# Gate and beta rows as broadcast loads behind the first weights, and an order planned with another table of load times

## The chip, the cores and the metric

The kernel runs on one core of one Trainium2 chip. The metric is the device time of one execution in microseconds, the median of several runs. Five engines take part: PE (TensorE, matrix products), DVE (VectorE), ACT (ScalarE), POOL (GpSimd) and SP (SyncE, which here issues nearly all DMAs).

## The reference, cut to what matters

The input `x` has 2048 tokens of width 512. The output mixes two branches token by token with a gate:

```
g = sigmoid((x * gate_w).sum(-1))            # one number for each token
a = A(x)        # attention with a memory, 32 heads of 16, four segments of 512 tokens
b = ((x @ W_gate) * (x @ W_gate > 0) * (x @ W_up)) @ W_down      # width 1792 between
out = g * a + (1 - g) * b
```

In each segment, branch A does causal attention within the segment (softmax of `q k / 4`), and from the second segment on reads a memory: `a_mem = phi(q) M / (phi(q) z + 1e-6)`. Here `M` and `z` are sums over the earlier segments of `phi(k) v` and `phi(k)`, and `phi(t)` is `t + 1` where `t > 0` and `exp(t)` elsewhere. The two are mixed by `sigmoid(beta)`, one number for each head, and then multiplied by `wo`.

So the gate row `gate_w` (512 numbers) is needed on all 128 partitions, since tokens lie on partitions when a token's gate is summed up; `beta` (32 numbers) is needed on all partitions too.

## The kernel before, in words

Everything stays in SBUF. The tokens are taken in four segments `s` of 512. For each there are projections (`proj`: `q`, `k` and `v`, four groups of four full 128x128x512 matmuls each), attention (`att`), memory update and reading (`mu`, `nd`), the two wide products with `W_gate` and `W_up` (`ffn`, 14 blocks of 128 columns) and the output product (`outp`), which adds up the attention part (`wo`) and the wide part (`wd`) in one accumulator.

`att` computes scores in groups called quads: matmuls that use the array as four row tiles of 32 and write all four banks of the PSUM tensor `psL`. One `exp` on ACT then turns the four banks into a tile of `E`, and POOL masks its diagonal blocks. The values (`pv`) use row tiles of 64 and write two banks of the other PSUM tensor, `psA`. Four banks of `psA` serve all accumulators; each is taken by a group of matmuls and is free again once its reader on DVE or ACT has copied it out.

The order of the work is not written down by hand. `program` describes every operation as an `Op` with the names that it reads and writes, a duration in nanoseconds and sometimes an earliest time (`after`). `Sched` then plays the work through with these durations and fixes, engine by engine, the order in which it is emitted and the semaphores that each instruction waits for. What counts for the change:

- `Sched.place` gives the time at which it believes that a DMA has landed. Operations that read the data are ready from then on.
- `Sched.jitter` adds a pseudo-random offset to the readiness of each operation, from a seed. The seeds change with PE's planned time, so each choice of seeds is another order.
- An engine executes its instructions in the emitted order. What is planned too early waits in its place, and what stands behind it waits too.

The names that the change touches: `touch` loads a few bytes early; `load` queues a weight load on SP or ACT; `load_gu(0)` and `load_gu(1)` load the first and second halves of the columns of `W_gate` and `W_up` (8 loads of 224 KB each); `load_x(c)` loads and transposes segment `c` of `x` into `xT`. `wo` and `wd` are loaded later, in one DMA each. `braw` holds `beta`, and `eb`, `romgh` and others are made of it. `gwb` is the gate row on 128 partitions.

In the kernel before, the gate row comes by a one-row DMA on ACT's queue into `oTt`. A matmul with a column of ones (`gwx`, L590) writes it to all partitions of a bank of `psL`, and ACT copies it to `gwb` (`gwc`, L592). The gates of segment 0 are four reductions on DVE (L620) that read the tiles `hT0` to `hT3`, which hold rows of `x` in the beginning. For the later segments a row tile is loaded into `osb` (`ldxr`, L625) and reduced (L628), one after the other, since they share a buffer. From a segment's four sums come `gexp` and `omg` on ACT and DVE; `gexp` is written to DRAM (`gscr`) and read back in another layout (`gexpT`, four DMAs), which `rdg` (L829) needs ahead of each attention output.

Other lines that the prediction names: L484 is the line of all plain loads, L506 of the transposing loads of `x`, L549 to L581 transpose segment 0, L655 is the exp of `phi`, L673 the `q` and `k` products, L671 `v`, L696 the transposes of `phik`, L721 adds up the memory, L743 to L745 read it, L757 makes `vsh` (a copy of the values shifted by 64 partitions), L775 are the quads, L781 the exps, L786 the masks, L809 the value products, L819 their transposes (`Tn`), L874 the wide products, L882 and L883 their relu (`rl`) on ACT or DVE, L885 the product that gives `hT`, L906 and L913 the output products.

Of the kernel before, what the change touches and what calls it, by code (L numbers as in the profile page):

```python
# [8 lines left out]
ACT = mybir.ActivationFunctionType  # L9
# [4 lines left out]

LAT = 60.0
MU_G = 1
PE_LAT = 175.0
SWITCH = 100.0
GATE_T = {1: 44000.0, 2: 90000.0, 3: 140000.0}
# [13 lines left out]

def t_pool(n, rate=1.0):
    return 160.0 + 0.975 * n * rate


PORT = ("kmask", "qts", "kts", "qphi", "kphi", "rdg", "ad", "oa", "gate", "omg1", "vone", "romgh", "epsv", "pmb")
# [59 lines left out]
class Sched:  # L98
# [178 lines left out]
    def place(self, op, e, start):  # L277
        op.eng = e
        if op.ep is not None and op.role == "w" and op.ep.bank is None:
            for ep in op.ep.group:  # L280
                bi, _ = self._bank_choice(op, e)
                for i in range(bi, bi + ep.nb):
                    if self.bank_ep[i] is not None:
                        op.preds += [(r, False) for r in self.bank_ep[i].readers]
                    self.bank_ep[i] = ep
                ep.bank = bi
        if e == "pool" and self.yield_to is not None:
            op.preds.append((self.yield_to, False))
            self.yield_to = None
        deps = {}  # L290
        for p in self._pred_done(op, e):
            deps[p.stream] = max(deps.get(p.stream, 0), p.idx)
        self._waits(e, deps)
        occ = op.occs[e]
        op.base = occ
        if e == "dve" and op.port:
            if self.pool_from <= start < self.now["pool"]:
                occ += self.now["pool"] - start
                self.yield_to = op
            self.port_free = start + occ  # L300
        if e == "pool":
            if start > self.now["pool"] + 1.0:
                self.pool_from = start
        if e == "pe":
            if op.mode != self.mode or start > self.now[e] + 60.0:
                occ += SWITCH
            self.mode = op.mode
        if op.dma:
            d = min(range(self.ndma), key=lambda i: (self.dma_end.get(i, 0.0), i))
            st = f"dma{d}"  # L310
            if self.cnt[st] > 0:
                self._waits(e, {st: self.cnt[st]})
            self.cnt[st] += 1
            self.semval[st, self.cnt[st]] = self.semval.get((st, self.cnt[st] - 1), 0) + 16 * op.nd
            inc = 16
            issued = start + occ
            self.dma_busy = max(self.dma_busy, issued) + op.nbytes / 340.0
            op.end = self.dma_busy + (1400.0 if start < 16000.0 else 5200.0 if start < 60000.0 else 3200.0)
            self.dma_end[d] = op.end
        else:  # L320
            st = e
            self.cnt[st] += 1
            inc = 1
            op.end = start + occ + op.lat
        idx = self.cnt[st]
        self.prog[e].append(("ins", op, st, inc))
        op.stream, op.idx, op.start, op.done = st, idx, start, True
        sn = dict(self.know[e])
        sn[st] = max(sn[st], idx)
        self.snap[st][idx] = sn  # L330
        self.now[e] = start + occ
        self.busy[e] += occ
        self.log.append((start, start + occ, e, op.name))
# [1 line left out]
    TOL = {"pe": 400.0, "act": 150.0, "dve": 250.0, "pool": 300.0, "sp": 300.0}  # L335

    def jitter(self, op):
        seed = self.seeds[min(int(self.now["pe"] / 34000.0), len(self.seeds) - 1)]
        j = self.jit.get((op.cidx, seed))
        if j is None:  # L340
            j = self.jit[op.cidx, seed] = random.Random(seed * 100003 + op.cidx).random() * 400.0
        return j

    def _choose(self, e):
# [15 lines left out]
        now = self.now[e]  # L360
        rdy = [h for h in heads if h[1] <= now + 20.0]
        if rdy:
            best = min(rdy, key=lambda h: (h[0], h[1] + self.jitter(h[2])))
            return best[2], best[1]
        hmin = min(heads, key=lambda h: (h[1], h[0]))
        best = hmin
# [60 lines left out]
def build_kernel(nc, A_x, A_wq, A_wk, A_wv, A_wo, A_beta, W_g, W_u, W_d, gate_w, out):  # L427
    _, S, D = A_x.shape
    F = W_g.shape[1]
    assert D == 512 and S % 512 == 0 and F % 128 == 0  # L430
    NSEG, KT, NF, NT = S // 512, D // 128, F // 128, S // 128
    EPS, SCALE = 1e-6, 16 ** -0.5
    sc = Sched(seeds=(52936,98560,17166,30259,57195,44848,1710,92264))
    T = {}
    with contextlib.ExitStack() as stack:
        for name, shape, dt in plan(S, D, F):
            T[name] = stack.enter_context(nc.sbuf_tensor(name, shape, dt))
        PL = stack.enter_context(nc.psum_tensor("psL", [128, 4, 512], F32))
        PA = stack.enter_context(nc.psum_tensor("psA", [128, 4, 512], F32))
        for st in sc.streams:  # L440
            sc.sem[st] = stack.enter_context(nc.semaphore(f"s_{st}"))
        program(sc, nc, T, PL, PA, A_x, A_wq, A_wk, A_wv, A_wo, A_beta, W_g, W_u, W_d, gate_w, out, NSEG, KT, NF, NT, EPS, SCALE)
        with nc.Block() as block:
            sc.emit(block)
    return sc


def program(sc, nc, T, PL, PA, A_x, A_wq, A_wk, A_wv, A_wo, A_beta, W_g, W_u, W_d, gate_w, out, NSEG, KT, NF, NT, EPS, SCALE):
# [31 lines left out]

    lact, lsp = [], []

    def load(eng, names, dst, src, nbytes, occ=460.0):
        (lact if eng == "act" else lsp).append(dma(eng, lambda e, dst=dst, src=src: e.dma_start(dst, src), nbytes, occ=occ, writes=names, name="ld" + names[0]))  # L484
    x0 = A_x[0, 0:512, :].rearrange("(i p) d -> p i d", p=128)
    def touch(n, src):
        load("act", ["adT"], V.adT[0:16, 32 * n:32 * n + 32], src, 1024)
    touch(0, A_wq[0:16, 0:32])
    load("act", ["oTt"], V.oTt[0:1, :], gate_w.rearrange("(a n) -> a n", a=1), 1024)
    for i in range(4):  # L490
        load("sp", [f"hT{i}"], V.hT[:, i, :], x0[:, i, :], 1 << 17)
    for nm, w, src in (("wq", V.wq, A_wq), ("wk", V.wk, A_wk), ("wv", V.wv, A_wv)):
# [11 lines left out]
    def load_x(c):  # L504
        for kt in range(KT):
            lsp.append(dma("sp", lambda e, c=c, kt=kt: e.dma_start_transpose(V.xT[:, kt, c * 512:(c + 1) * 512], A_x[0, c * 512:(c + 1) * 512, kt * 128:(kt + 1) * 128]),  # L506
                           1 << 17, occ=1280.0, writes=[f"xT{c}_{kt}"], name=f"ldx{c}_{kt}"))
    load("sp", ["braw"], V.braw[:], A_beta.partition_broadcast(128), 8192)
    load_gu(0)
    load_gu(1)  # L510
    load_x(1)
    sc.queue(0, lact)
# [19 lines left out]
    st = []  # L532
# [54 lines left out]
            ins = e.matmul(A(epw)[:, 0:n], lhsT=nc.const_aps.tensor(1.0, [128, 128], BF16), rhs=nc.const_aps.tensor(1.0, [128, n], BF16), start=True, stop=True)  # L587
        return ins
    xps.append(pe(warm1, 380, name="warm1", ep=epw, role="w"))
    xps.append(pe(lambda e: e.matmul(PL[:, 2, :], lhsT=nc.const_aps.tensor(1.0, [128, 128], BF16)[0:1, :], rhs=V.oTt[0:1, :], start=True, stop=True), 300, reads=["oTt"], writes=["bankL2"], name="gwx"))  # L590
    xps[-1].after = 6400.0
    xcs.append(act(lambda e: e.activation(V.gwb[:], PL[:, 2, :], ACT.Copy), t_act(512), reads=["bankL2"], writes=["gwb"], name="gwc"))  # L592
    sc.queue(0, xps)
    sc.queue(0, [t for t in xcs if t.eng == "dve"])
    sc.queue(0, [t for t in xcs if t.eng == "act"])
# [112 lines left out]
    def mu(s):  # L708
# [3 lines left out]
        def fn(e):  # L712
# [4 lines left out]
                                       rhs=V.vaug[:, s % 2, tt, 8 * G + 2 * j:8 * G + 2 * j + 2, :].rearrange("q h c -> q (h c)"),  # L717
                                       start=(tt == 0), stop=(tt == 3), tile_position=(0, 32 * j), skip_group_check=True)
            return ins
        m = pe(fn, 300.0, reads=[f"phik{g}" for g in range(4)] + va(s), name=f"mu{s}", ep=ep, role="w", mode="c")  # L720
        d = dve(lambda e: e.tensor_tensor(V.Mc[:], V.Mc[:], A(ep)[:, 0:136].rearrange("q (g c) -> q g c", g=4), ALU.add), t_dve(136), reads=["Mc"], writes=["Mc"], name=f"mum{s}", ep=ep, role="r")  # L721
        ps = []
        for G in range(4):
# [305 lines left out]
```

## Time and profile before

| what | value |
|---|---|
| median of 3 runs | 264.92 us (264.72, 264.92, 266.2) |
| profiled execution | 264.76 us, its span 263.0 us |
| PE busy | 254.4 us, 97% of the span, 2714 matmuls |
| ACT, DVE, POOL busy | 188.7, 181.5, 119.5 us |
| DMA | 19.23 MB, mean 73 GB/s; 135 to 379 GB/s in the first 33 us |
| granted TensorE clock | full speed |

The span is what the profiler sees from the first to the last record; the 1.8 us beside it are start and end of the execution. PE's busy time counts matmuls whose ends are modelled, so it is read for where it has holes, not for its rate. The records of a few matmuls are missing from the trace, mostly the first after a change of form. In a group's line the columns are: line, engine, operation, output <- input, count; in a timeline: start, duration, engine, line, operation, and in brackets the idle time ahead and what ended it.

### The profile page before, as it was taken

What the parts mean: (1) busy time and instruction counts of PE and PEld (TensorE: products, weight loads), DVE (VectorE), ACT (ScalarE), POOL (GpSimd) and SP (SyncE); (2) the same over time, 40 slices, a digit from 0 to 9 for tenths busy, and PEclk for the clock granted to TensorE, in tenths of its full rate; (3) what the DMA queues carried; (4) which work ended last, traced back from release to release, by engine and by line L of the source; (5) the groups of instructions that cost most, each with busy time, mean ns of one, the idle gap of its engine ahead of it and who ended that gap; (6) DMA issues with size and microseconds to landing.
All of it is one profiled execution on the core that took longest, in us unless ns stands there. A gap on an engine that the chain in (4) does not pass through costs nothing.

```text
span 263.0 us, 6637 instructions
## 1 busy us (share of the span) xinstructions
PE 254.4 (97%) x2714; PEld 113.1 (43%) x2748; DVE 181.5 (69%) x359; ACT 188.7 (72%) x167; POOL 119.5 (45%) x283
## 2 busy tenths in 40 slices
PE   7999999999999999999999999999999999999996
PEld 3444444434444443534444434444444434344444
DVE  5788887977886388876887954868582636657600
ACT  4597898599878789588886777787677657767021
POOL 3025544764545366764446265634344453535100
PEclk9999999999999999999999999999999999999999
DMA  6899666982041341510032320100034120000011
GB/s 182 223 379 209 135 83 80 286 146 57 20 106 23 75 68 44 82 40 4 0 87 64 80 62 23 21 4 2 0 92 55 22 60 22 0 2 1 4 40 40
DMA packets 34528, 19.23 MB, mean 73 GB/s; under 512 B 24001, under 2 KB 33986, under 8 KB 34498
## 3 DMA queue, kind: packets, MB, share of 16 engines
q1 hardware_dynamic: 34368, 18.80, 32.0%
q8 instruction: 21, 0.34, 0.6%
q14 instruction: 9, 0.07, 0.1%
q10 hardware_dynamic: 130, 0.01, 0.0%
HBM read 9.75 MB, written 2.11 MB: 45 GB/s over the span
## 4 chain that ended last, share of the span: by engine, by line
PE 94%; issue 2%; DVE 1%; DMA 1%; SPq 0%; ACT 0%; DVEq 0%
PE psA L874 37%; PE psA L913 19%; PE psA L673 11%; PE psL L775 9%; PE psA L809 7%; PE psA L906 5%; PE psA L671 5%; PE psA L736 1%; DMA hT<-in_A_x_dram 1%; PE psA L716 1%; DVE vaug L699 0%; SPq L484 0%; DVE phiq L657 0%; ACT xT L581 0%; DVE osb L922 0%
## 5 line engine op out<-in xcount | busy, mean ns | idle before, releaser
L786 POOL TENSOR_SCALAR_AFFINE_SELECT E<-E 64x256 bf16<-64x256 bf16 (+1 forms) x256 | 111.8, 446 | 122.2 <-ACT E L781 100.9
L781 ACT ACTIVATE E<-psL 128x2048 bf16<-128x2048 f32 x72 | 135.1, 1876 | 33.8 <-PE psL L775 31.1
L874 PE MATMUL psA<-xT,wg 128*128 128x512 bf16 x212 | 57.0, 380 | 1.9 <-issue 1.6
L874 PE MATMUL psA<-xT,wu 128*128 128x512 bf16 x219 | 58.0, 380 | 0.7 <-issue 0.5
L913 PE MATMUL psA<-wd,hT 128*128 128x512 bf16 (+2 forms) x229 | 52.2, 366 | 1.1 <-issue 1.0
L885 DVE TENSOR_TENSOR hT<-psA,rl 128x512 bf16<-128x512 f32 x56 | 38.2, 681 | 13.6 <-PE psA L874 11.3
L819 DVE STREAM_TRANSPOSE Tn<-psA 128x512 f32<-128x512 f32 x32 | 21.3, 696 | 20.0 <-PE psA L809 20.0
L913 PEld LDWEIGHTS psA<-wd,hT 128*128 128x128 bf16 x238 | 21.4, 98 | 23.7 <-issue 1.9
L874 PEld LDWEIGHTS psA<-xT,wu 128*128 128x128 bf16 x224 | 20.6, 98 | 25.3 <-issue 1.5
L874 PEld LDWEIGHTS psA<-xT,wg 128*128 128x128 bf16 x224 | 20.0, 98 | 24.9 <-issue 3.9
L775 PE MATMUL psL<-qT,kp 32*128 32x192 bf16 (+7 forms) x512 | 28.5, 287 | 0.0
L882 ACT ACTIVATE rl<-psA 128x512 bf16<-128x512 f32 x32 | 19.1, 597 | 10.2 <-PE psA L874 9.5
L775 PEld LDWEIGHTS psL<-qT,kp 32*128 32x128 bf16 x512 | 8.2, 92 | 29.9 <-issue 15.3
L923 ACT ACTIVATE osb<-psA,omg 128x512 bf16<-128x512 f32 (+1 forms) x12 | 8.1, 679 | 17.9 <-PE psA L906 14.0
L883 DVE TENSOR_SCALAR rl<-psA 128x512 bf16<-128x512 f32 x24 | 16.7, 696 | 3.2 <-PE psA L874 2.5
L809 PE MATMUL psA<-E,vaug 64*17 64x128 bf16 (+7 forms) x512 | 18.7, 283 | 0.0
L809 PE MATMUL psA<-E,vsh 64*17 64x128 bf16 (+7 forms) x512 | 18.3, 283 | 0.0
L673 PE MATMUL psA<-xT,wq 128*128 128x512 bf16 x62 | 16.2, 380 | 0.5 <-ACT xT L581 0.3
L906 PE MATMUL psA<-wo,oT 128*128 128x512 bf16 (+2 forms) x67 | 16.2, 366 | 0.2 <-issue 0.2
L673 PE MATMUL psA<-xT,wk 128*128 128x512 bf16 x61 | 16.0, 380 | 0.4 <-issue 0.3
L671 PE MATMUL psA<-wv,xT 128*128 128x512 bf16 x62 | 14.7, 380 | 0.3 <-issue 0.3
L809 PEld LDWEIGHTS psA<-E,vaug 64*17 64x17 bf16 x512 | 11.6, 86 | 6.0 <-issue 3.6
(76 smaller groups left out, 214.9 us busy)
## 6 DMA issues: line engine op xcount, KB each, us to landing
vsh<-vaug SPq DMA_DIRECT2D x8, 272.0 KB, 3.8
out_dram<-osb SPq DMA_DIRECT2D x15, 128.0 KB, 1.7
wg<-in_B_W_gate_dram SPq DMA_DIRECT2D x8, 224.0 KB, 5.7
wu<-in_B_W_up_dram SPq DMA_DIRECT2D x8, 224.0 KB, 5.9
wd<-in_B_W_down_dram SPq DMA_DIRECT2D x1, 1792.0 KB, 10.0
osb<-in_A_x_dram SPq DMA_DIRECT2D x12, 128.0 KB, 2.2
hT<-in_A_x_dram SPq DMA_DIRECT2D x4, 128.0 KB, 2.4
wq<-in_A_wq_dram SPq DMA_DIRECT2D x4, 128.0 KB, 2.8
```

Of the source, the lines that this page charges most:

```text
L671: ins = e.matmul(A(ep)[:, :], lhsT=V.xT[:, kt, tok + col * 128:tok + (col + 1) * 128], rhs=w[:, kt, :], start=(kt == 0), stop=(kt == KT - 1))
L673: ins = e.matmul(A(ep)[:, :], lhsT=w[:, kt, col * 128:(col + 1) * 128], rhs=V.xT[:, kt, tok:tok + 512], start=(kt == 0), stop=(kt == KT - 1))
L775: ins = q.matmul(PL[:, jj, o:o + 512 - 64 * c], lhsT=V.kp[r, kslot(s, G), c, :], rhs=V.qT[r, qslot(s, G), 64 * c:512], start=True, stop=Tr ...
L781: acts.append(act(lambda a: a.activation(V.E[:, e, :, :], PL[:, :, :], ACT.Exp, scale=SCALE), t_act(2048), reads=[f"bankL{b}" for b in ran ...
L786: pools.append(pool(lambda g, ap=ap, base=base: g.affine_select(out=ap, in_=ap, compare_op=ALU.is_ge, fill=0.0, base=base, pattern=[[0, 4] ...
L809: ins = q.matmul(A(eps[p])[32 * jj:32 * jj + 17, 64 * c:512], lhsT=v[:, 8 * G + 2 * jj + p, :], rhs=V.E[r, e, jj, o:o + 512 - 64 * c], sta ...
L819: ds.append(dve(lambda e, p=p, ep=eps[p]: e.transpose(V.Tn[:, p, :], A(ep)[:, :]), t_dve(512), writes=[f"Tn{p}"], name=f"tr{s}_{G}_{p}", e ...
L874: ins = e.matmul(A(ep)[:, :], lhsT=w[:, kt, f * 128:(f + 1) * 128], rhs=V.xT[:, kt, c * 512:(c + 1) * 512], start=(kt == 0), stop=(kt == K ...
L882: evs.append(sc.add(Op([("act", lambda e, ep=eg, r=r: e.activation(V.rl[:, r, :], A(ep)[:, :], ACT.Relu), t_act(512)), ("dve", lambda e, e ...
L885: evs.append(dve(lambda e, ep=eu, r=r, hs=hs: e.tensor_tensor(V.hT[:, hs, :], A(ep)[:, :], V.rl[:, r, :], ALU.mult), t_dve(512), reads=[f" ...
L906: ins = e.matmul(A(ep)[:, 0:c1 - c0], lhsT=V.oT[:, o0 + G, i * 128:(i + 1) * 128], rhs=V.wo[:, G, c0:c1], start=st_ and G == 0, stop=sp_ a ...
L913: ins = e.matmul(A(ep)[:, 0:c1 - c0], lhsT=V.hT[:, slots[f], i * 128:(i + 1) * 128], rhs=V.wd[:, f, c0:c1], start=st_ and f == f0, stop=sp ...
```

## The change

It does three things. The one-row load, the matmul L590 and the copy L592 go; instead the gate row is loaded with one DMA that reads it for each of the 128 partitions. This DMA and that of `beta` stand behind the eight loads of `load_gu(0)`, where `beta`'s stood ahead of them. And the planner gets other numbers: a table `dma_time` with a service time and a latency for each kind of DMA, by which a load counts as landed 0.25 us after its service, in place of a rate with 1.4, 5.2 or 3.2 us on top; 490 in place of 300 ns for `mu`, 472 in place of 460 ns for an issue; sixteen seeds for 17 us each instead of eight for 34 us; and, for one operation in ten, an offset to its priority too. So from about 13 us on the whole emitted order is another one, with the same operations.

```diff
+STRETCH = 17000.0
+BUMP = 2.2
+BUMP_P = 0.1
...
+def dma_time(op):
+
+    n = op.name
+    for px, svc, lat in (("ldhT", 546, 1650), ("ldwq", 546, 1650), ("ldwk", 546, 1650), ("ldwv", 546, 1650), ("ldwg0_0", 1400, 1650), ("ldwg", 596, 1650), ("ldwu", 596, 1650),
+                         ("ldbraw", 1600, 1650), ("ldgwb", 1000, 1650), ("ldxr", 400, 1700), ("ldx", 560, 2000), ("kT2", 560, 2000), ("aT", 560, 2000), ("vsh", 850, 2300),
+                         ("ldwo", 1750, 1650), ("ldwd", 6100, 1650), ("st", 400, 1400), ("gwr", 50, 1700), ("grd", 100, 1900)):
+        if n.startswith(px):
+            return svc, lat
+    return op.nbytes / 300.0, 1650
...
-            self.dma_busy = max(self.dma_busy, issued) + op.nbytes / 340.0
-            op.end = self.dma_busy + (1400.0 if start < 16000.0 else 5200.0 if start < 60000.0 else 3200.0)
+            svc, lat = dma_time(op)
+            self.dma_busy = max(self.dma_busy, start + lat) + svc
+            op.end = self.dma_busy + (0.0 if start < 8000.0 else 250.0)
...
     def jitter(self, op):
-        seed = self.seeds[min(int(self.now["pe"] / 34000.0), len(self.seeds) - 1)]
+        seed = self.seeds[min(int(self.now["pe"] / STRETCH), len(self.seeds) - 1)]
         j = self.jit.get((op.cidx, seed))
         if j is None:
-            j = self.jit[op.cidx, seed] = random.Random(seed * 100003 + op.cidx).random() * 400.0
+            r = random.Random(seed * 100003 + op.cidx)
+            j = self.jit[op.cidx, seed] = (r.random() * 400.0, BUMP if r.random() < BUMP_P else 0.0)
         return j
...
-            best = min(rdy, key=lambda h: (h[0], h[1] + self.jitter(h[2])))
+            best = min(rdy, key=lambda h: (h[0] + self.jitter(h[2])[1], h[1] + self.jitter(h[2])[0]))
...
-    sc = Sched(seeds=(52936,98560,17166,30259,57195,44848,1710,92264))
+    sc = Sched(seeds=(20535,46112,39258,56108,387,36564,95759,69596,46532,65787,16279,44074,61783,45860,67077,4305))
...
-    def load(eng, names, dst, src, nbytes, occ=460.0):
+    def load(eng, names, dst, src, nbytes, occ=472.0):
...
     touch(0, A_wq[0:16, 0:32])
-    load("act", ["oTt"], V.oTt[0:1, :], gate_w.rearrange("(a n) -> a n", a=1), 1024)
...
+    load_gu(0)
     load("sp", ["braw"], V.braw[:], A_beta.partition_broadcast(128), 8192)
-    load_gu(0)
+    load("sp", ["gwb"], V.gwb[:], gate_w.partition_broadcast(128), 1 << 17)
     load_gu(1)
...
-    xps.append(pe(lambda e: e.matmul(PL[:, 2, :], lhsT=nc.const_aps.tensor(1.0, [128, 128], BF16)[0:1, :], rhs=V.oTt[0:1, :], start=True, stop=True), 300, reads=["oTt"], writes=["bankL2"], name="gwx"))
-    xps[-1].after = 6400.0
-    xcs.append(act(lambda e: e.activation(V.gwb[:], PL[:, 2, :], ACT.Copy), t_act(512), reads=["bankL2"], writes=["gwb"], name="gwc"))
...
-        m = pe(fn, 300.0, reads=[f"phik{g}" for g in range(4)] + va(s), name=f"mu{s}", ep=ep, role="w", mode="c")
+        m = pe(fn, 490.0, reads=[f"phik{g}" for g in range(4)] + va(s), name=f"mu{s}", ep=ep, role="w", mode="c")
```

Lines behind the table stand 13 to 16 higher in the new file: the quads are L788 there, the `q` and `k` products L686, the reductions of later segments L641.

## The prediction, made before the changed kernel ran

> **What bounds the kernel now.** I began with the page's chain that ended last and its row of PE slices.
>
> ```profile
> PE   7999999999999999999999999999999999999996
> ...
> PE 94%; issue 2%; DVE 1%; DMA 1%; SPq 0%; ACT 0%; DVEq 0%
> ```
>
> TensorE is busy from its second slice to the last and carries 94% of the chain, so a change pays only by shortening the matmul stream and costs only where it makes that stream stop. Next come the waits of PE alone (total us, times, longest us).
>
> ```profile
> PE psA L874 <- issue: 2.1, 13, 0.2
> PE psA L673 <- ACT xT L581: 0.3, 1, 0.3
> PE psA L874 <- DVE vaug L699: 0.2, 1, 0.2
> PE psA L874 <- DVE rdm L744: 0.2, 1, 0.2
> ```
>
> No wait for another engine is longer than 0.3 us, and those at all add up to about 1 us. The old order has practically no stall left to remove. Third, the timeline of the start, where the change removes something.
>
> ```profile
> 5.66 1.02 PE L673 MATMUL psA<-xT,wq 128*128 128x512 bf16 x4 [0.27 <-ACT xT L581]
> 6.62 0.39 PE L590 MATMUL psL<-oTt,const-bfloat16-1.0 1*128 1x512 bf16 x1
> 6.93 2.76 PE L673 MATMUL psA<-xT,wq 128*128 128x512 bf16 x12
> 7.04 0.60 ACT L592 ACTIVATE gwb<-psL 128x512 bf16<-128x512 f32 x1 [1.45 <-PE psL L590]
> 7.67 0.69 DVE L620 CUSTOM_DVE_ANT_0 hT<-hT,gwb 128x512 bf16<-128x512 bf16 x1 [2.15 <-ACT gwb L592]
> ```
>
> The spread of the gate row (L590) stands between projections; the four gate reductions L620 follow at 7.67 to 12.4, while DVE is half idle. Fourth, SP's timeline and the landing of the load named in the fourth line (a query of its tile from 46 to 48 us).
>
> ```profile
> 17.09 5.71 SPq L506 DMA_TRANSPOSE xT<-in_A_x_dram  x4
> ...
> 40.67 1.95 SPq L637 DMA_DIRECT2D gexpT<-gscr  x4
> 45.77 0.51 SPq L484 DMA_DIRECT2D wd<-in_B_W_down_dram  x1
> 46.32 2.90 SPq L625 DMA_DIRECT2D osb<-in_A_x_dram  x1
> ```
> ```profile
> DMA to landing us min/median/max: 9.9/9.9/9.9
> ```
>
> The `wd` load leaves at 45.77; the first row load of segment 1 (`ldxr4`, into `osb`) queues behind its 1.8 MB and lands at 46.32 + 9.9 = 56.2. Last, who uses it, from the timelines of DVE and PE:
>
> ```profile
> 57.20 0.68 DVE L628 CUSTOM_DVE_ANT_0 osb<-osb,gwb 128x512 bf16<-128x512 bf16 x1
> ```
> ```profile
> 54.66 1.04 PE L673 MATMUL psA<-xT,wq 128*128 128x512 bf16 x4
> 55.53 1.03 PE L874 MATMUL psA<-xT,wg 128*128 128x512 bf16 x4
> ```
>
> In the old order this reduction (`gate4`, L628) stands where DVE comes at 57.2, one us after the row is there.
>
> **The spread goes.** Full matmuls start 0.216 us apart (the four at 5.66 end their pitch at 6.52), yet the next one starts at 6.93: L590 costs 0.41 us of the stream. The weights behind it do not take that back: by the trace's landing records `wq` part 2 is there at 6.6 and part 3 at 6.95, needed at 6.95 and 7.6 in the new order. The ACT copy L592 and the one-row DMA lay in idle time: nothing.
>
> **The new order.** The rest of the diff re-draws the whole order. The program says how often PE goes from full matmuls into the row-tiled forms (scores, values, memory update): 74 times before, 73 after. One entry costs 0.10 us (two full matmuls at 28.11 end their pitch at 28.54, the scores start at 28.64). Everything else on PE is the same set of instructions (the plan's new prices for `mu` and for an issue change where things stand, not how long they take). So without any stall the new order saves 0.41 + 0.10 = 0.5 us; that is the most that I can find for it.
>
> **Where it can stop: loads.** `beta` moves behind the eight first-half weights, the gate row comes after it. On SP each issue takes 0.47 us; `beta`'s is only moved, the new one puts all later issues 0.47 us back. In the queue the 128 KB broadcast takes between 0.35 us (128 packets over 16 engines at the 46 ns that 1 KB packets took in the packet records) and 1.6 us (the gap that `beta`'s 128 packets left between the landings of `wv` at 11.3 and `beta` at 12.9); I take 0.7, nearer to the equally large packets of the projection weights, which land 0.52 us apart. The first user is `gate0`, on DVE behind the first `hT` product. That product is at 19.4 before, so about 19.0 now, and `gate0` is reached at 19.7. The row lands about 19.0 (18.2, where the last of the eight landed, plus 0.7): no wait, 0.8 if `beta`'s price is met twice. The transposed tiles of segment 1 land 0.7 later than 26.5 (issue 21.27 plus 5.2), at 27.2; PE wants them at 27.25 - 0.41 = 26.84. That is a stall of 0.4 (0 to 1.3).
>
> `beta` now lands near 18.3. Its user `eb` stands on ACT behind the first relu (18.7) and ahead of the third exp, so it costs its own 0.23 us, as before. The four gate reductions, 0.69 us each, leave idle DVE time for 19.7 to 31, where DVE was busy 7.65 of the 9 us from 17 to 26: 2.8 us more work ahead of products that free banks. By the rows that is between nothing (the free tenths take it) and 0.7 (one reduction in the way); I take nothing, since whatever PE loses ahead of 56 us is inside the next item. With them `gexp`, the `gscr` write and `gexpT`'s read move; the read, four issues of 0.47, would land near 38, its user `rdg` on DVE comes after the first transposed values at about 40 (46.2 before).
>
> [...]
>
> **Where it can stop: the wd load.** The new table `dma_time` lets the plan count a load as there 0.25 us after its service, where the old one added 3 to 5 us. It moves the users forward. In the new program `gate4` comes right after the `hT` product of the `wu` group that PE ends at about 53.5 (counted from 54.66 back: one full matmul, two score groups with 0.33 each, three entries, and the 0.41). DVE is there at 54.4. Behind `gate4` on DVE stand a relu (`rl`) and a transpose `Tn`; the `wq` group 12 full matmuls beyond the point 54.66 waits for that relu, because it takes its bank. Unstalled that group starts at 54.66 + 12 x 0.216 - 0.10 - 0.41 = 56.74.
>
> When does `ldxr4` land now? SP has the same issues ahead of `wo` as before, plus 0.47 for the gate row. Also `gexpT`'s read now follows `gscr`'s write at once: the write lands 1.5 us after an issue of 0.6, 0.9 us of waiting that two transposes covered before. Against that, one transpose issue of 1.97 us at 34.19 (1.26 is usual) need not recur: minus 0.7 or nothing. So 0.7 to 1.4 later; I take 1.1, that is 57.3. `gate4` starts at 57.4, holds DVE 0.6, the relu takes 0.7 and PE sees it at 58.85: 2.1 us after 56.74. The earlier stall at 27 us is inside this one, since the landing does not move with PE. With SP no later than before it is 1.0; with another 1.0 of blocked issue it is 3.1. Below nothing it can't be.
>
> The kernel's in-order engines make this price. In the trace DVE waited 2.2 us for `gwb` with its next instructions behind it. [...]
>
> The same load also delays the two `phik` transposes that ACT's `ek` (L668 of the new file) waits for ahead of an exp: they landed 0.5 and 1.0 us behind `ldxr4` before, so 58.3 now; `ek` 1.05 and exp 1.88 end at 61.3. The scores that need it stand 12 full matmuls behind 56.74 plus a product group, so at 59.4, or 61.5 after the stall: covered by it, and 1.9 if the stall were not there.
>
> **Sum.** Against the profiled execution (264.76, span 263.0): -0.5 + 2.1 gives 266.4. Its time is 0.16 below the median of the three runs, so 264.92 + 1.6 = 266.5.
>
> **Rivals.** *SP runs as planned, and wd is in time.* If no issue were blocked, SP would save the 0.8 (first `vsh`), 1.45 (`phik` at 24.89, 2.7 instead of 1.26) and 0.7 it lost in the old trace, and `ldxr4` would land at 54.7, with DVE. Then only the stall at 27 us remains: 264.4 to 265.3. For it: these blocks depend on what lies in the queue. Against: the queue is as full as before, by 128 KB more. It decides when the row lands by 55.3. *The gate row is late.* `gate0` would hold DVE at 20 us for 0.8 and PE's next banks with it; alone 265.2, and inside the later stall otherwise. *More of the same later.* The shorter allowance holds for every DMA: `Tn`-to-output chains, `amemT` and the other eleven rows. Each hit costs a few tenths and the first may cost 3.1: 267.0 to 268.5. Nothing in the old trace shows one, as its users came late. *Faster*: it needs 0.8 us more than I can find in a stream whose waits are under 0.3; only if the slice at either end got shorter.
>
> **Chances.** A measurement of this kernel can tell about 0.5%, 1.3 us: 263.6 and 266.24 are the bounds. My case, 265.6 to 267.0: 0.46, some six tenths of it above 266.24. SP as planned: 0.22. Gate row late: 0.07, below the bound. More later: 0.22. Faster: 0.03. So slower is 0.28 + 0.22 = 0.50, faster 0.03, the same the remaining 0.47. The range from 264.4 (no stall) to 268.0 leaves out the faster case and the far end of "more later", about one in ten; the unknown SP delay alone spans 265.4 to 267.5.
>
> **What would show it.** Right: no L590, 73 entries; PE waits of 0.2 to 0.6 us near 27; the row of segment 1 landing near 57.3, DVE idle some 3 us ahead of L641, PE idle about 2 us ahead of a `wq` matmul (L686) near 57 to 59. Wrong: that row landing before 55, or DVE reaching `gate4` later than I count; PE idle near 20 would be the gate row; PE idle spread over the later segments would be the third rival.

## The result, and the profile after

The changed kernel took 268.91 us in the median of six runs (267.09 to 269.87), the kernel before 264.92 on the same chip: a ratio of 1.0134, interval 1.0091 to 1.0177. Ratios are of mean times, so they differ a little from those of the medians, and leave out single executions that were more than 1.5% above the fastest of their kernel. That is slower by more than the 0.5% that can be told, which the prediction held for slightly likelier (0.50) than no change (0.47); the time is above the range's end of 268.0, and the loss of 4.0 us is two and a half times the 1.6 forecast. The profiled execution took 269.87 us, span 268.1, so it shows the upper end of the six runs.

The page's row of PE slices, the granted clock and the chain that ended last:

```profile
PE   8999999959999999999999999999999999999996
PEclk9999999997999999999999999999999999999999
...
PE 89%; DMA 5%; SPq 4%; DVE 1%; issue 0%; DVEq 0%
```

Of 40 slices of 6.7 us, PE is half idle in the ninth, and in the tenth the granted clock falls. The chain now holds 5% of DMA. The waits of PE (total us, times, longest us) name one stall, where before there were only tenths:

```profile
PE psA L686 <- DVE rl L896: 3.8, 1, 3.8
...
PE psL L585 <- DMA hT<-in_A_x_dram: 0.4, 1, 0.4
```

At the start the spread is gone; PE's timeline has the 16 `wq` matmuls in one piece, where four, L590 and twelve stood:

```profile
5.86 3.61 PE L686 MATMUL psA<-xT,wq 128*128 128x512 bf16 x16
```

SP's timeline, and from the page's list of DMA issues the line of `wd` (its end is the us from issue to landing):

```profile
12.81 0.43 SPq L500 DMA_DIRECT2D gwb<-in_gate_w_dram  x1
...
47.56 1.62 SPq L500 DMA_DIRECT2D wd<-in_B_W_down_dram  x1
49.22 1.79 SPq L638 DMA_DIRECT2D osb<-in_A_x_dram  x1
51.11 8.32 SPq L709 DMA_TRANSPOSE phik<-ek  x4
```
```profile
wd<-in_B_W_down_dram SPq DMA_DIRECT2D x1, 1792.0 KB, 11.6
```

`wd` leaves at 47.56 instead of 45.77 and takes 11.6 us instead of 10.0; its issue holds SP for 1.62 us where it was 0.51. The row behind it, issued at 49.22, landed at 59.54 by the landing records, and the first two `phik` transposes at 60.02 and 60.52. Its users, on the timelines of DVE and of PE, and the stretches 57.1 to 67.2 us (busy time of PE, PEld, DVE, ACT, POOL, then the granted clock, DMA share, GB/s):

```profile
53.80 0.69 DVE L898 TENSOR_TENSOR hT<-psA,rl 128x512 bf16<-128x512 f32 x1
59.56 0.69 DVE L641 CUSTOM_DVE_ANT_0 osb<-osb,gwb 128x512 bf16<-128x512 bf16 x1 [5.07 <-DMA osb<-in_A_x_dram]
60.18 0.69 DVE L896 TENSOR_SCALAR rl<-psA 128x512 bf16<-128x512 f32 x1
```
```profile
56.72 0.40 PE L788 MATMUL psL<-qT,kp 32*128 32x320 bf16 x8
60.92 1.89 PE L686 MATMUL psA<-xT,wq 128*128 128x512 bf16 x4 [3.81 <-DVE rl L896]
```
```profile
57.10:60.40 3.30, 0.02 (x4) 0.00 (x0) 0.84 (x3) 0.00 (x0) 0.07 (x1) 1.00 1.42 146
60.40:63.80 3.40, 2.88 (x7) 1.03 (x8) 3.21 (x6) 3.21 (x3) 2.63 (x7) 0.50 0.29 77
63.80:67.20 3.40, 3.40 (x19) 1.39 (x18) 2.29 (x6) 2.54 (x3) 1.66 (x4) 1.00 0.11 39
```

DVE stands 5.07 us ahead of `gate4`, with the relu `rl` behind it. PE is free at 57.05 (the quads at 56.72 hold it 0.33) and starts `wq` at 60.92, 3.87 us later. Then it runs 7 matmuls in 2.88 us, which at full pitch (0.216 us each) take 1.5: another 1.4 us, because the clock is at 0.50 from 60.4 to 63.8. The sum is -0.5 + 3.87 + 1.4 = 4.8 of the span's 5.1; the projections also start 0.2 later (5.86 for 5.66). Of the six runs three show a mean clock of 0.994 (269.43, 269.70, 269.87) and three of 1.00 (267.09, 267.82, 268.40): a stretch of 3.41 us at half clock takes just 0.006 off the mean, so it goes with the slower three, and 2.2 to 3.5 us of loss are there without it. In e1 below the two groups overlap (268.01 at 0.994, 268.91 at 1.00), so the stretch is not all that makes runs differ.

### The profile page after: what moved, and what is told of

It reads as the page before. It is cut to its first block, busy times and chain, and to the rows that moved or that the text cites. A ratio compares the mean times of both kernels' runs of the same rounds, so it can differ in the third digit from the quotient of the medians.

```text
span 268.1 us, 6660 instructions
## 1 busy us (share of the span) xinstructions
PE 260.5 (97%) x2747; PEld 114.1 (43%) x2747; DVE 184.3 (69%) x361; ACT 187.3 (70%) x164; POOL 120.4 (45%) x283
## 4 chain that ended last, share of the span: by engine, by line
PE 89%; DMA 5%; SPq 4%; DVE 1%; issue 0%; DVEq 0%
PE psA L887 35%; PE psA L926 19%; PE psA L686 9%; PE psL L788 8%; PE psA L822 6%; PE psA L919 5%; PE psA L684 4%; DMA osb<-in_A_x_dram 4%; SPq L521 2%; PE psA L749 1%; SPq L500 1%; DMA hT<-in_A_x_dram 1%; SPq L709 1%; DVE Tn L832 0%; PE psA L729 0%
## 5 line engine op out<-in xcount | busy, mean ns | idle before, releaser
L799 POOL TENSOR_SCALAR_AFFINE_SELECT E<-E 64x256 bf16<-64x256 bf16 (+1 forms) x256 | 113.0, 451 | 124.8 <-ACT E L794 93.4
L887 PE MATMUL psA<-xT,wu 128*128 128x512 bf16 x224 | 59.3, 381 | 0.0
L887 PE MATMUL psA<-xT,wg 128*128 128x512 bf16 x224 | 59.2, 380 | 0.0
L926 PE MATMUL psA<-wd,hT 128*128 128x512 bf16 (+2 forms) x238 | 55.4, 367 | 0.0
L788 PE MATMUL psL<-qT,kp 32*128 32x192 bf16 (+7 forms) x512 | 28.6, 287 | 0.0
L895 ACT ACTIVATE rl<-psA 128x512 bf16<-128x512 f32 x26 | 15.5, 598 | 12.7 <-PE psA L887 12.7
L896 DVE TENSOR_SCALAR rl<-psA 128x512 bf16<-128x512 f32 x30 | 20.6, 686 | 3.7 <-PE psA L887 2.6
L788 PEld LDWEIGHTS psL<-qT,kp 32*128 32x128 bf16 x512 | 8.2, 92 | 30.0 <-issue 17.4
L686 PE MATMUL psA<-xT,wq 128*128 128x512 bf16 x64 | 17.0, 395 | 3.8 <-DVE rl L896 3.8
L686 PE MATMUL psA<-xT,wk 128*128 128x512 bf16 x64 | 17.4, 388 | 0.0
L684 PE MATMUL psA<-wv,xT 128*128 128x512 bf16 x64 | 15.5, 380 | 0.0
L935 DVE TENSOR_SCALAR osb<-psA,omg 128x512 bf16<-128x512 f32 (+1 forms) x6 | 4.1, 682 | 15.9 <-PE psA L919 11.0
## 6 DMA issues: line engine op xcount, KB each, us to landing
wd<-in_B_W_down_dram SPq DMA_DIRECT2D x1, 1792.0 KB, 11.6
```

Source lines behind the costliest of these rows:

```text
L684: ins = e.matmul(A(ep)[:, :], lhsT=V.xT[:, kt, tok + col * 128:tok + (col + 1) * 128], rhs=w[:, kt, :], start=(kt == 0), stop=(kt == KT - 1))
L686: ins = e.matmul(A(ep)[:, :], lhsT=w[:, kt, col * 128:(col + 1) * 128], rhs=V.xT[:, kt, tok:tok + 512], start=(kt == 0), stop=(kt == KT - 1))
L788: ins = q.matmul(PL[:, jj, o:o + 512 - 64 * c], lhsT=V.kp[r, kslot(s, G), c, :], rhs=V.qT[r, qslot(s, G), 64 * c:512], start=True, stop=Tr ...
L799: pools.append(pool(lambda g, ap=ap, base=base: g.affine_select(out=ap, in_=ap, compare_op=ALU.is_ge, fill=0.0, base=base, pattern=[[0, 4] ...
L887: ins = e.matmul(A(ep)[:, :], lhsT=w[:, kt, f * 128:(f + 1) * 128], rhs=V.xT[:, kt, c * 512:(c + 1) * 512], start=(kt == 0), stop=(kt == K ...
L896: ("dve", lambda e, ep=eg, r=r: e.tensor_scalar(V.rl[:, r, :], A(ep)[:, :], 0.0, None, ALU.max), t_dve(512))],
```

## The experiments

All but e9 and e10 keep the changed kernel's order on every engine and move, split or add single instructions after planning; e9 and e10 are planned anew, with other seeds. The code cuts leave out what `...` marks and the bookkeeping of the semaphores. `cut` takes an instruction with its waits out of SP's program, `paste` puts it ahead of (or behind) another. Ratios are against the kernel before on the same chip, whose medians were 264.82 (e1 to e4), 265.11 (e5 to e8) and 264.89 (e9 to e11).

**e1: the row ahead of wd.**

```diff
     sc.run()
+    paste(cut("ldxr4"), "ldwo")
```

> The changed kernel with one instruction moved after planning: SP issues the first row load of segment 1 (ldxr4) ahead of wo and wd. Every other instruction stands where it stood. Theory 1 (whatever lies behind wd stops PE, and two things do): the row now lands near 50, gate4 no longer waits, but the two phik transposes that ACT's ek (L668) waits for still land near 60.0 and 60.5, so ek ends at 61.6, its exp at 63.5, and PE wants that exp's bank at 59.4 when nothing held it before. A stall of about 4.1 us by another wait (ACT in place of DVE), the time stays at 267 to 269.5. Theory 2 (the gate reduction alone carries the loss, the exp is hidden): 264.2 to 264.8.

Measured: 268.92 us, ratio 1.0148 (1.0112 to 1.0184), the same loss as the change. The row landed at 49.82, and the stall has another name, by ACT's timeline and PE's waits:

```profile
60.29 1.06 ACT L668 ACTIVATE ek<-kT 128x1024 bf16<-128x1024 bf16 x1 [3.84 <-DMA phik<-ek]
61.25 1.86 ACT L794 ACTIVATE E<-psL 128x2048 bf16<-128x2048 f32 x1
```
```profile
PE psL L788 <- ACT E L794: 3.4, 1, 3.4
```

ACT stands 3.84 us ahead of `ek`, the exp behind it ends at 63.1, and PE waits 3.4 us for its bank. Theory 1 holds: two waits stood side by side behind `wd`, and taking one away alone brings nothing.

**e3: half of wd ahead of the row.**

```diff
+    op.fns["sp"] = lambda e: e.dma_start(V.wd[:, 0:7, :], src[:, 0:7, :])
...
+    paste(wd, "ldxr4")
+    paste([("ins", two, st, inc)], "ldxr7", behind=True)    # two: blocks 7 to 13
```

> The changed kernel with wd in two DMAs: blocks 0 to 6 where wd stood, ahead of ldxr4, blocks 7 to 13 behind the last row load of segment 1 (ldxr7, about 64 us), long before their use near 75. A dose: half the bytes ahead of the row. Theory 1 (time goes by the landing of what queues behind, and the granted clock falls only after an idle of about 4 us): 0.9 MB less at 350 GB/s is 2.6 us, so the row lands near 56.9, rl is seen by PE near 58.4 where PE is free at 56.74: a stall of 1.7 us, no stretch at half clock; 264.3 + 1.7 = 266.0, range 265.3 to 266.6. Theory 2 (the loss hangs on the issue of SP or on the order, not on the bytes of wd): 267.5 or more. Theory 3 (row and transposes come in time as soon as the queue is half as long): 264.3.

Measured: 265.98 us, ratio 1.0032 (1.0012 to 1.0053), mean clock 1.0 in all twelve runs.

```profile
PE psL L788 <- ACT E L794: 1.2, 1, 1.2
...
PE psA L686 <- DMA xT<-in_A_x_dram: 0.6, 1, 0.6
```

The row landed at 56.29 (56.9 expected); the stall behind `wd` is 1.2 us, again by the exp, since the transposes landed at 58.34 and 58.74. Fewer bytes in front, less loss: that part of theory 1 is shown. Its 350 GB/s is near what the queue moved with `wd` in it in the kernel before (353 to 368 GB/s from 48 to 54 us). That the clock falls only after an idle of about 4 us is not shown: in the changed kernel's profile it fell 3.35 us into the stall of 3.87 (57.05 to 60.40), in e10 below 2.5 us into one of 3.0. That its time is met within 0.1 us is partly luck, since the stall is 1.2 and not 1.7, and half the bytes took 8.1 us from issue to landing, not half of 11.6. A second wait, 0.6 us for the transposed tiles of segment 1, makes up the rest; it is the one that the prediction had put at 27 us.

**e2: row, wo and wd ahead of the transposing loads of segment 3.**

```diff
+    for n in ("ldxr4", "ldwo", "ldwd"):
+        paste(cut(n), "ldx3_0")
```

> The changed kernel with three loads moved on SP after planning: ldxr4, wo and wd are issued ahead of the four transposing loads of segment 3 (which PE needs far later), near 41.7 instead of 47 to 49 us. Nothing else moves. Theory 1 (the whole loss comes from what queues behind wd at 49 to 60 us): wd lands near 52, the phik transposes near 54 to 55, DVE meets gate4 at 54.4 with its row there, no wait of PE over 0.3 us is left, full clock throughout; 264.76 - 0.5 = 264.3, range 264.0 to 264.7, which would be 0.2% under the kernel before. Theory 2 (the new order has further stalls that the first one covers, or the broadcast of the gate row holds something near 20 us): 265.0 or more, with PE idle elsewhere. Should the transposes of segment 3 suffer behind wd and be late for their matmuls near 80 us, a wait would show there.

Measured: 266.12 us (265.87 to 266.69), ratio 1.0043 (1.0028 to 1.0057). Theory 1 missed by 1.8 us. PE's timeline shows where:

```profile
51.69 0.22 PE L822 MATMUL psA<-E,vsh 64*17 64x128 bf16 x3
53.02 0.22 PE L822 MATMUL psA<-E,vsh 64*17 64x128 bf16 x5 [1.10 <-issue]
```

Eight value matmuls of one operation are torn apart after the third; no semaphore wait stands between them. `wd` landed at 53.01. The packet records hold a packet of 16384 bytes of an instruction queue from 50.53 to 51.66 here, and in the profiles of the changed kernel, e1, e3, e5, e6 and e8 the same block starts between 47.62 and 48.05. So this block of instructions came some 2.6 us later than usual, while `wd` was in the queue (issued at 42.60; the page has 260 GB/s in the slice from 46.2 to 52.8). What is shown is that the stall is gone in e5 and e6, where the order is the same and `wd` is not in the queue then. That late instructions are what stopped PE is argued from the times and not shown: no view names the engine whose queue it is, and the packet had ended 1.36 us before PE went on. The move also blocked SP: the four transposing loads behind `wd` took 9.73 us to issue instead of 5.2, and `phik` landed at 57.35, not at 54 to 55.

**e5: wd in three parts, where the queue is nearly idle.**

```diff
+    parts = ((0, 5, "ldxr5"), (5, 10, "ldxr6"), (10, 14, "ldxr7"))
...
+        p = Op([("sp", lambda e, a=a, b=b: e.dma_start(V.wd[:, a:b, :], src[:, a:b, :]), 472.0)], name=f"ldwd{n}")
+        paste((wd[:-1] if n == 0 else []) + [("ins", p, st, inc)], name, behind=True)
```

> The changed kernel with wd in three DMAs (blocks 0 to 4, 5 to 9, 10 to 13), each behind one of the row loads ldxr5, ldxr6, ldxr7 on SP, at about 57, 61 and 65 us, where the DMA queue is nearly idle and the first use is near 80. Everything else stands where it stood. Theory 1 (the loss is the 1.8 MB in one piece and nothing else in the new order): ldxr4 and the phik transposes land with 2 to 3 us of latency, no wait of PE behind 30 us is left, full clock; 264.76 - 0.5 = 264.3, with 0 to 0.7 at 27 us for segment 1's transposed tiles (met in two of the four runs so far): 264.1 to 264.9. Theory 2 (the stall of e2, 1.3 us inside a group of value matmuls near 51.7 with no wait in the program, belongs to the order and not to the load that was in the queue at that moment): it appears here too, and the time is 265.4 to 266.2.

Measured: 265.34 us (264.20 to 266.72), ratio 1.0009 (0.9983 to 1.0036), 0.4 above the expected range. The stalls behind `wd` and that of e2 are gone:

```profile
PE psA L686 <- DMA xT<-in_A_x_dram: 0.4, 1, 0.4
PE psL L585 <- DMA hT<-in_A_x_dram: 0.3, 1, 0.3
```

What is left is the wait at 27 us, 0.4 us in this profile. So the one load in that place made the loss of the change, to within the interval; theory 2 falls by the trace, since its stall is not there, while the median by itself is next to its 265.4.

**e6: also the transposing loads of segment 1 ahead of the second halves.**

```diff
+    for n in range(4):
+        paste(cut(f"ldx1_{n}"), "ldwg1_0")
```

> Kernel e5, and the four transposing loads of segment 1 stand on SP ahead of the second halves of wg and wu instead of behind them. Theory (what is left at 27 us is those tiles landing at 26.8 to 27.5): they land near 22 to 24, the wait of the first q products of segment 1 goes, the second halves land 3 to 5 us later, by 28, far ahead of their first use near 50; 0 to 0.7 less than e5, mean about 0.3: 263.9 to 264.5, under the kernel before. Rival: the transposes hold SP, the second halves and the first phik transposes come late, and it is no better or slower than e5.

Measured: 264.49 us, eleven of twelve runs between 264.11 and 264.84 (one 266.83), ratio 0.9983 (0.9958 to 1.0008). The last three tiles landed at 20.30 to 21.16, in e5 at 26.15 to 27.26, and PE no longer waits at 27 us. Between e5 and e6 lie 0.85 us in the median, and e5's scatter of 2.5 us is gone with them but for the one run. e6's median is 0.6 us under the kernel before; the interval still holds 1.

**e4 and e7: the spread put back** (into e2 and into e6).

```diff
+        e.matmul(PL[:, 2, :], lhsT=nc.const_aps.tensor(1.0, [128, 128], BF16)[0:1, :], rhs=one[0:1, :], start=True, stop=True)
         return fn0(e)
```

> Kernel e2 (three loads early on SP) with one matmul more between the first projections, of the form that the change removed: a column of ones times a row of 512, contraction over 1 partition, into the bank of psL that it used before; its result is read by nobody. It puts back the removed spread alone. The prediction's step: 0.41 us more than e2 (0.22 for its 512 columns at full pitch, 0.2 for going in and out of the one-row form). Rival: the loads at the start bound the projections, and it costs nothing, 0.0 to 0.1.

> Kernel e6 with the spread put back: one matmul of a column of ones times a row of 512 between the first projections, as in e4. The prediction's first term alone, now with nothing behind it to hide it: 0.41 us more than e6, or 0.2 to 0.3 where the second part of wq lands late enough to cover some of it (in e4 the trace showed 0.32 from its start to the next matmul). Rival: 0, since the loads set the start.

Measured: e4 265.77 us, ratio 1.0041 (1.0017 to 1.0065); e7 264.80, ratio 1.0002 (0.9982 to 1.0021).

```profile
5.87 1.05 PE L686 MATMUL psA<-xT,wq 128*128 128x512 bf16 x4
6.85 0.39 PE L1046 MATMUL psL<-const-bfloat16-1.0 1*128 1x512 bf16 x1
7.17 1.04 PE L686 MATMUL psA<-xT,wq 128*128 128x512 bf16 x4
```

e7 is 0.31 us above e6; its trace has the four matmuls of 5.87 end their pitch at 6.73 and the next start at 7.17. e4 decides nothing, since the weight load and the matmul more on PE also moved the point of e2's torn group: that stall is not there, and a wait of 0.6 us for the exp takes its place.

**e8: more bytes ahead of the row.**

```diff
+    two = Op([("sp", lambda e: e.dma_start(V.wdx[:], src[:, 0:4, :]), 472.0)], name="ldwd2")
...
+    paste(wd + [("ins", two, st, inc)], "ldxr4")
```

> The changed kernel with one load more: behind wd and ahead of ldxr4, SP also loads blocks 0 to 3 of wd a second time into a buffer that nobody reads, 0.52 MB. Dose upward. Theory 1: 1.5 us more in front of the row (0.52 MB at 350 GB/s), the stall of PE grows from 4.1 to 5.6, and the granted clock then falls in every run instead of in half of them, at the same price of 1.3 to 1.5 us: 268.9 + 1.5 + 0.7 = 271.1, range 270.3 to 272; mean granted clock 0.994 in all runs. Rival (the stretch at half clock grows with the idle time): more than 3.5 us at half clock. Rival (the bytes do not matter): 268.9.

Measured: 269.88 us (268.09 to 271.13), ratio 1.0177 (1.0141 to 1.0214), below the expected range. In the profile the row landed at 59.50, not 1.5 us later than in the changed kernel: `wd` itself was there at 57.44, so the 0.52 MB fitted into the time that the changed kernel's profile had lost. The mean clock is 0.994 in three of four runs and 1.0 in one, not in all. In the profile the stretch at 0.50 lasts 3.41 us, as in the changed kernel's. So the dose upward decides nothing: the interval overlaps that of the change (1.0091 to 1.0177), and the transfer of `wd` varies from profile to profile by as much as these 0.52 MB were to cost (9.9 us here and 11.6 in the changed kernel's, for 1.5). That the bytes count rests on e3 and e5.

**e9: one price in the table.**

```diff
-                         ("ldwo", 1750, 1650), ("ldwd", 6100, 1650), ("st", 400, 1400), ("gwr", 50, 1700), ("grd", 100, 1900)):
+                         ("ldwo", 1750, 1650), ("ldwd", 12900, 1650), ("st", 400, 1400), ("gwr", 50, 1700), ("grd", 100, 1900)):
...
-    sc = Sched(seeds=(20535,46112,39258,56108,387,36564,95759,69596,46532,65787,16279,44074,61783,45860,67077,4305))
+    sc = Sched(seeds=(20535,46112,39258,96657,93487,64596,83145,40222,14806,27325,24007,20555,23396,20288,96170,9853))
```

> The changed kernel with one entry of the planner's table of load times altered: wd's service 12.9 us in place of 6.1, which puts its planned landing at 59.3, where it was measured at 59.1 (12.9 is the planned queue of 46.2 up to 59.1). The first three seeds stay, so the order up to about 51 us is the same; the later seeds were searched anew for a plan as short as the old one (261.3 us planned, 261.2 before), so the order behind is another. SP issues as in the changed kernel; gate4 now stands on DVE at 59.8 of the plan instead of 54.8, ek on ACT at 61.8 instead of 56.4. Theory (the one wrong price is the cause, not the broadcast and not the order as such): no wait of PE behind wd, full clock, what is left is the floor and the 0 to 0.8 at 27 us: 264.3 to 265.6. Rival (wd's own price is right but every load of the new plan is too early): further waits, 267 or more.

Measured: 265.05 us (264.41 to 266.18), ratio 1.0001 (0.9978 to 1.0024). PE has no wait over 0.3 us behind its first instruction, the clock is full. The loads are as late as in the changed kernel: the row landed at 59.45, the first two transposes at 59.94 and 60.43. But DVE now comes to `gate4` at 59.65, from other work and without a wait:

```profile
59.05 0.68 DVE L695 CAST qT<-psA 128x512 bf16<-128x512 f32 x1
59.65 0.77 DVE L641 CUSTOM_DVE_ANT_0 osb<-osb,gwb 128x512 bf16<-128x512 bf16 x1
```

So late loads cost nothing where the plan puts their users behind them, and the entry for `wd` carries the loss; the rest of the table, the bumps and the new price of `mu` carry none that shows here. Two limits: the later seeds differ too, and no run has other seeds with the old entry; and 12.9 is not `wd`'s own service, as it also makes up for the time by which SP is behind its plan.

**e10: the first part of the change alone, under the old rule for loads.**

```diff
-    sc = Sched(seeds=(52936,98560,17166,30259,57195,44848,1710,92264))
+    sc = Sched(seeds=(21862,32683,14240,45390,47492,27027,34141,79845))
...
-    load("act", ["oTt"], V.oTt[0:1, :], gate_w.rearrange("(a n) -> a n", a=1), 1024)
...
+    load_gu(0)
     load("sp", ["braw"], V.braw[:], A_beta.partition_broadcast(128), 8192)
-    load_gu(0)
+    load("sp", ["gwb"], V.gwb[:], gate_w.partition_broadcast(128), 1 << 17)
...
```

> The kernel before with the first part of the change alone: the gate row and beta as broadcasts behind the first halves, no spread, no copy; the planner's old rule for loads stays (seeds searched anew, 260.4 us planned). The old rule believes the gate row there at 16.6 us, and gate0 stands on DVE there; measured it lands at 19.7. Theory (a load planned too early holds an in-order engine and what stands behind it): DVE idles some 3 us ahead of gate0 from 16.7 to 19.7, its copies out of PE's banks stand behind it, PE stops for 1.5 to 3 us near 18 to 20, and the time is 265.8 to 267.5; no wait behind wd, since the old rule allows for it (gate4 at 56.2 may wait a few tenths). Rival (DVE's idle time covers it): 264.2 to 264.8.

Measured: 268.48 us (266.26 to 271.04), ratio 1.0105 (1.0048 to 1.0161), more than expected. The lines of the matmul `gwx` and the copy `gwc` go here too. The timelines of DVE, ACT and PE:

```profile
20.06 0.69 DVE L617 CUSTOM_DVE_ANT_0 hT<-hT,gwb 128x512 bf16<-128x512 bf16 x1 [3.85 <-DMA gwb<-in_gate_w_dram]
```
```profile
18.91 0.23 ACT L594 ACTIVATE eb<-braw 128x32 f32<-128x32 bf16 x1 [3.70 <-DMA braw<-in_A_beta_dram]
19.99 1.86 ACT L778 ACTIVATE E<-psL 128x2048 bf16<-128x2048 f32 x1
```
```profile
21.90 0.61 PE L772 MATMUL psL<-qT,kp 32*128 32x256 bf16 x8 [3.01 <-ACT E L778]
23.27 1.78 PE L871 MATMUL psA<-xT,wu 128*128 128x512 bf16 x4
```

DVE waits 3.85 us for the gate row, as expected, and ACT 3.70 us for `beta` (landed at 18.88), with an `ek` and the exp that PE needs behind `eb`; this second wait, which the expectation did not name, is the one that releases PE after 3.0 us. Then four `wu` matmuls take 1.78 us instead of 1.04: half clock again, from 21.38 to 24.79, left out of the expectation too. So both rows, where the change puts them, are too late for the old rule, and the new table is what gives their users a later place; the same table is too early for what stands behind `wd`.

**e11: e6 with two of the first loads on ACT's queue.**

```diff
+    for n in (3, 1):
+        (item,) = cut(f"ldhT{n}")
+        item[1].fns["act"] = item[1].fns["sp"]
+        sc.prog["act"].insert(0, item)
```

> Kernel e6 with two of the four loads of x's first tiles (hT1 and hT3) issued on ACT's queue instead of SP's, ahead of the first small load there; nothing else moves. It asks whether the rest of the scatter, 0.3 to 0.9 us ahead of the first projections, comes from the issue of the first loads, 0.47 us each on SP. Theory: hT3 lands near 3.8 instead of 4.4 to 4.7, wq's parts up to 0.9 earlier, the projections start 0.3 to 0.6 earlier, 264.0 (263.8 to 264.3). Rival: the loads share the same engines and land together no earlier, or ACT's first copy is held by the issues: 264.4 to 264.8.

Measured: 264.55 us (264.15 to 265.18), ratio 0.9975 (0.9947 to 1.0003); against e6 nothing. `hT3` landed at 4.55 instead of 4.41 although it was issued 0.96 us earlier. The rival holds in that the load landed no earlier; that shared engines are the reason is not shown.

## Why the prediction was right in kind and wrong in size

**The floor, right.** The spread was put at 0.41 and measured at 0.31 (e7 against e6). Without late loads the new order was to be 0.5 us under the old one; e6 is 0.6 under it, e5 with the wait at 27 us 0.2 above. Since e6's interval holds 1, this fits the floor and does not prove it.

**The gate row, right by luck.** It was to land at 19.0 with 0.7 us in the queue; it landed at 19.67, 1.06 behind `beta`, and DVE came to `gate0` at 19.70. No single price fits: in the other kernels' profiles the row landed 0.2 us (e11) to 1.8 us (e8) behind `beta`. e10 shows what late rows cost when the plan gives their users no later place: 3 us and the clock, there by way of `beta`; what the late gate row would cost by itself was not tried.

**The stall at 27 us, right as a term.** In the profile the tiles landed at 26.80 and PE did not wait. e3 and e5 waited 0.6 and 0.4, and e6 without it gains 0.85 in the median, for a term of 0.4 (0 to 1.3). That it lies inside the later stall of the changed kernel is argued, not tried.

**Beta and gexpT, without effect.** `beta` landed at 18.61 and `eb` ran at 18.65. `gexpT` landed at 41.20, 3 us behind the estimate, and `rdg` ran at 41.42 with no wait of PE.

**The wait behind wd: right mechanism, wrong landing.** `gate4`, the relu behind it and the `wq` group were the chain named, DVE came to `gate4` at 54.49 (54.4), PE was free at 57.05 (56.74). The step that failed is "I take 1.1, that is 57.3": the row landed at 59.54, 3.35 us later than before. Of the 2.2 us missed, 0.7 is issue (`wd` left 1.79 later, not 1.1: SP was already 1.6 behind at the first transposing load, 18.66 for 17.09) and 1.5 is the transfer, 11.58 us for 10.04, which the step took over unchanged. In the eight profiles in which `wd` goes in one piece its transfer took 9.9 to 11.6, so the profiled execution is at the slow end; by the issue alone the stall would be 2.8, which gives 267.2 as an estimate, near the fastest of the six runs (267.09). The upper bound of 3.1 held only more blocked issue, no longer transfer, and so the range ended too early. The second user was right too: "1.9 if the stall were not there" became 3.4 in e1, by the same later landing.

**The clock, missing.** This is the second step that failed: the sum had a stall and no price for what comes after it. The profile's 3.41 us at 0.50 cost 1.4 us. The half-clock stretches of the changed kernel, e8 and e10 are 3.41 us each, and the full-clock stretches ahead of them are 16, 16 and 5 times that; full clock sets in at 3.7 to 6.1 us of the span, earlier or later from kernel to kernel. Counted from there in windows of 3.41 us, these are the windows ahead of the stretch in the changed kernel and in e10, and the two over which e1's stall lies (columns as above; PE's busy time is the first):

```profile
56.99:60.40 3.41, 0.13 (x8) 0.00 (x0) 0.84 (x3) 0.00 (x0) 0.07 (x1) 1.00 1.49 152
```
```profile
17.97:21.38 3.41, 0.93 (x5) 0.20 (x2) 1.32 (x4) 2.47 (x3) 0.00 (x0) 1.00 0.93 305
```
```profile
58.33:61.74 3.41, 1.48 (x7) 0.49 (x5) 0.74 (x2) 1.45 (x2) 0.00 (x0) 1.00 0.74 160
61.74:65.16 3.42, 1.99 (x12) 0.90 (x13) 1.90 (x4) 3.42 (x4) 1.60 (x4) 1.00 0.12 38
```

The stall of e10, 3.0 us, fell with 2.5 us into one window, PE was busy for 0.93 us of it, and the granted clock went to 0.50. The stall of e1, 3.4 us, was longer but lay across two windows with 1.48 and 1.99 us of work, and the clock stayed full; in four of e1's six runs it did not (mean clock 0.993 to 0.994). So the length of the stall alone does not part these profiles, and its place in the windows does; that the clock goes by such windows is the author's reading of these lengths and not shown. In e10 a stall of 3.0 us was enough: the prediction's own bound of 3.1 already called for a term of up to 1.4 us.

**The rivals.** "SP runs as planned" fell: SP was 4.3 us behind its plan at `wd` (47.56 for 43.26). "More of the same later" fell: behind 64 us no wait of PE is on the list, though the same allowance of 0.25 us holds there.

## What to carry to other kernels

A planner whose prices for loads were right to 0.2 us at the start can still be wrong later, where the issuing engine has fallen behind its plan and one load is much larger than the rest: here planned and measured landings agreed within 0.2 us from 13 to 27 us, and at `wd` the measured one was 6.6 late (59.13 for 52.54): 4.3 of it is SP's delay, 2.3 the time from issue to landing (11.6 for 9.3 in the plan). The one large load carried the error to the loads queued behind it (the row at 59.54, the transposes at 60.02 and 60.52). Cut a large load with a far-off use into parts and put them where the queue is idle (e5: 265.34 us for 268.91; the changed kernel's queue moved 77 and then 39 GB/s from 60.4 to 67.2 us); look for all waits behind it before removing one, since the second was nearly as long as the first (3.4 us in e1 for 3.8). And price a stall of TensorE like those here, 3.0 us in e10 and 3.87 in the changed kernel, with up to 1.4 us on top, which is what the half clock cost in the changed kernel.

## What the runs showed of the hardware that was not expected

- A stall of 3.0 to 3.9 us went with 3.41 us at half clock in three profiles (changed kernel, e8, e10) and not in a fourth (e1), and in some runs of the same kernel and not in others; in the profiles, the busy share of a single window of 3.41 us parts the cases (0.13, 0.23 and 0.93 us of work, against 1.48).
- TensorE stopped for 1.1 us within one group of matmuls in e2, with no wait in the program, while a block of 16 KB of instructions came some 2.6 us later than usual behind a 1.8 MB load. Whether the late block is what stopped TensorE is open: in e4 the block came nearly as late (50.21) and this stop is not there.
- The 1.8 MB of `wd` took 11.58 us in the changed kernel's profile and 9.9 in e8's, which had the same order ahead of it. With the difference goes a spell from 50.5 to 53.5 us in which the 1 KB packets took 53 to 90 ns instead of 46 to 52 (half-microsecond means); an instruction packet of 8192 bytes in it took 1062 ns, in e3's spell 1227, and 309 to 371 in the profiles of the kernel before, e1 and e8. What slows the packets is open; no run here tells it.
